# One fused attention and MoE kernel: the order of the loads of W2 and v, and the place of one key-value product

## The chip, the cores, the metric

One core of a Trainium2 chip. Its engines go by short names: PE is TensorE (PEld its weight loads), DVE is VectorE, ACT is ScalarE, POOL is GpSimd, SP is SyncE. The metric is the device time of one execution in microseconds; smaller is better. Every profile is of one execution.

## The reference

Attention in linear form, then an MLP with ELU:

```python
q_s = softmax(q, axis=-1); k_s = softmax(k, axis=2)      # 8 batches, 8 heads, 576 rows, 64 columns
kv  = einsum('bhsd,bhse->bhde', k_s, v)                  # the key-value product
x   = einsum('bhsd,bhde->bhse', q_s, kv) ...             # to 4608 tokens x 512
out = elu(x @ w_in) @ w_out                              # 512 -> 2048 -> 512
```

## The kernel before

It works in nine blocks of 512 tokens. A "unit" is half a batch: units 0 and 1 are batch 0, units 2 and 3 batch 1. For each block PE runs `hg` (x @ w_in, 64 matmuls, line L654) and `out` (ELU result @ w_out, 64 matmuls, L700). The attention of the next batch goes between the `out` matmuls: transposes of q (L464), the key-value product (L491), two groups that apply it (L584, L618). The output of a block needs all of W2, in 16 chunks of 256 KB, and in block 0 W2 is still coming in, together with q, k and v of batch 1.

The loads of that stage, all issued in this order by GpSimd on one queue:

```python
W2CUT = (0, 4, 8, 12, 13, 14, 16)     # part 0: chunks 0-3, 1: 4-7, 2: 8-11, 3: chunk 12, 4: 13, 5: 14-15
for what in (0, "2q", "3q", 1, 2, "2k", "2v", "3k", 3, "3v", 4, 5):
    if isinstance(what, int):
        gp = self.load_w2(what, -50, follow=gp)
    elif what == "3v":
        for h in range(2):                      # v of unit 3 as two halves, 288 KB each
            gp = self.load_half(3, "v", h, -50, gp)
    else: ...                                   # 576 KB each
```

PE's order in block 0 is a list of 24 steps, four token tiles for each part of W2, with the attention of batch 1 hung behind some of them:

```python
if j == 0:
    work = dict(zip((6, 9, 15, 20), (
        lambda: self.tp(2, C, key), lambda: self.tp(3, Dd, key),   # transposes of q
        lambda: kv([2, 3]),                                        # key-value product of units 2 and 3
        first)))                                                   # first attention group
    plan = [(ts, W2CUT[s], W2CUT[s + 1]) for s in range(6) for ts in range(4)]
```

The product is one PE step of 72 small matmuls. It waits for k (after its exponential on ACT) and v (after a cast to bf16 on DVE) of both units:

```python
R = []
for n in units:
    i = n % 2
    R += [f"kR{i}", f"VB{i}0", f"VB{i}1", f"VBone{i}"]
S.add("pe", len(units) * 270 + 200, mm, key, R=R, X=self.banks(ps), tag=f"kv{units}")
```

The kernel's own list scheduler orders the instructions on the other engines by modelled times, so a change of one order can move others.

The softmax here doesn't subtract the row's maximum and nothing guards it: scores larger than these inputs give would overflow.

Of the kernel before, what the change touches and what calls it, by code (L numbers as in the profile page):

```python
# [257 lines left out]
class Gen:  # L258
# [482 lines left out]
    def program(self):  # L741
# [49 lines left out]
        self.hg_mm(0, 0, 3, (1,))  # L791
        self.hg_mm(0, 1, 2, (1,))
        self.ao_rest(0, 1, -60)
        for what in (0, "2q", "3q", 1, 2, "2k", "2v", "3k", 3, "3v", 4, 5):
            if isinstance(what, int):
                gp = self.load_w2(what, -50, follow=gp)
            elif what == "3v":
                for h in range(2):
                    gp = self.load_half(3, "v", h, -50, gp)
            else:  # L800
                gp = self.load(int(what[0]), what[1], "gp", -50, follow=gp)
# [6 lines left out]
        def loads(n, ts, key):  # L808
            for t in ts:
                self.ldq = self.load(n, t, "sp", key, after=self.w2, follow=self.ldq)  # L810
                self.w2 = ()

        def elem_q(b, key, dmat="sp"):
            for n in (2 * b, 2 * b + 1):
                self.q_part(n, key)
                if b != 2:
                    self.q_mul(n, key, dmat)

        def elem_k(b, key, vconv="gp"):
            for n in (2 * b, 2 * b + 1):  # L820
                self.k_part(n, key, "halves" if n == 3 else vconv)

        def convert(b, key):
            for n in (2 * b, 2 * b + 1):
                self.cvt(n, key)
# [3 lines left out]
        for j in range(NBLK):  # L829
            order = [A, Bs, C, Dd]  # L830
            for g in range(8):
                self.hg(j, g, order[g % 4], key, "gp" if j or g > 2 else "act" if g == 1 else "dve",
                        (0, 1, 2, 3) if j or g > 3 else (2, 3))
                key += 1
                if (j, g) == (0, 1):
                    for x in (2, 3):
                        self.hg_mm(0, x, order[x], (0, 1), key)
                if (j, g) == (0, 0):
                    elem_q(1, 8, None)
                    elem_k(1, 8, "dve")  # L840
            if j == 1:
                S.rel = self.pe
                for n in (4, 5):
                    self.q_mul(n, key, "sp")
                convert(2, key)
            b = j + 1
            more = b + 1 < B
            work = {}
            k1 = key + 14
            if b < B:  # L850
                n0, n1 = 2 * b, 2 * b + 1
                S.slack = 3500 if j else 1500
                if more:
                    loads(n0 + 2, "q", key)
                    loads(n1 + 2, "q", key)
                    S.rel = self.pe
                    if j:
                        elem_q(b + 1, k1)

                def kv(units, ps=C, more=more):  # L860
                    self.kv(units, ps, key)
                    for n in units:
                        if more:
                            loads(n + 2, "kv", key)
                            self.k_part(n + 2, k1)

                def aos(b=b, more=more, A=A, C=C, Dd=Dd):

                    small = int(self.split(b) >= 5)
                    self.ao(2 * b, 1 - small, Dd, key)  # L870
                    self.ao(2 * b + 1, 1 - small, A, key)
                    self.ao_rest(b, C, key, small)
                    if more:
                        convert(b + 1, k1)

                def first():
                    for n, ps in ((2, Dd), (3, C)):
                        self.ao(n, 0, ps, key, evac="split")

                if j == 0:  # L880
                    work = dict(zip((6, 9, 15, 20), (
                        lambda: self.tp(2, C, key), lambda: self.tp(3, Dd, key), lambda: kv([2, 3]),
                        first)))
                else:
                    work = dict(zip((5, 12) if j == 1 else (3, 10), (lambda: kv([n0, n1]), aos)))
            if j == 0:
                plan = [(ts, W2CUT[s], W2CUT[s + 1]) for s in range(6) for ts in range(4)]
            else:
                plan = [(ts + t, jj, jj + 4) for ts in (0, 2) for jj in range(0, 16, 4) for t in range(2)]
            if j == NBLK - 1:  # L890
                plan = plan[:8] + [(ts, jj, jj + 4) for ts in (2, 3) for jj in range(0, 16, 4)]
            bank = [2 * A, 2 * A + 1, 2 * Bs, 2 * Bs + 1]
            for k, (ts, jj0, jj1) in enumerate(plan):
                self.out_mm(j, ts, bank[ts], jj0, jj1, key)
                if jj1 == 16:
                    self.out_store(j, ts, bank[ts], key, last=j == NBLK - 1)
                if k in work:
                    work[k]()
                key += 8 / len(plan)
            if j == 0:  # L900
                S.rel = self.pe
                elem_q(2, k1)
                self.ao_rest(1, Dd, key)
            A, Bs, C, Dd = (Dd, C, A, Bs) if j else (C, Dd, A, Bs)
# [32 lines left out]
```

## Time and profile before

| | before |
|---|---|
| median of 3 runs | 298.45 us (298.19 to 298.48) |
| PE busy | 290.1 us, 98% of a span of 296.5 us |
| DVE, ACT, POOL busy | 51%, 51%, 41% |
| granted clock of PE, as a share of full speed | 1.000 |

The prediction below shows the lines. Three views carry it: the chain that ended last (what each step waited for, in order of time), the timeline of one engine (start, length, engine, line, operation, count, and in brackets the idle time before and what ended it), and the waits of ACT and DVE for loads, from which the landings are read.

### The profile page before, as it was taken

The numbers are of one execution on the slowest core, as the hardware profiler recorded it, in microseconds if no ns is written. First come the engines' busy times: TensorE is split into PE (matmuls) and PEld (weight loads), VectorE is DVE, ScalarE is ACT, GpSimd is POOL, SyncE is SP. The second block draws the span as 40 slices with busy tenths as digits, with TensorE's granted clock in tenths as the row PEclk, the third lists the DMA queues.
The fourth block names the chain that finished last, engine by engine and source line by source line (L and its number), as shares of the span: only waits on it lengthen the run. The fifth ranks groups of instructions, "written<-read, shape, count | busy, mean of one in ns | idle before, by whom it ended". The sixth has DMA issues, their size and how long they took to land.

```text
span 296.5 us, 4336 instructions
## 1 busy us (share of the span) xinstructions
PE 290.1 (98%) x1824; PEld 234.9 (79%) x1824; DVE 149.9 (51%) x167; ACT 151.9 (51%) x176; POOL 122.9 (41%) x133
## 2 busy tenths in 40 slices
PE   7999999999999999999999999999999999999995
PEld 2578778887888788878888888888888888888883
DVE  6757942988347903792268416760661056106600
ACT  5666367953676275536554555536531454135411
POOL 8998101662187035713472337314740055005500
PEclk9999999999999999999999999999999999999999
DMA  7999988928991597039902990099003110230022
GB/s 243 320 393 390 389 281 308 389 83 133 337 248 66 200 354 147 0 96 362 238 7 56 359 270 17 4 346 194 0 0 71 45 30 0 56 76 13 0 71 71
DMA packets 36515, 49.37 MB, mean 167 GB/s; under 512 B 16656, under 2 KB 17168, under 8 KB 36496
## 3 DMA queue, kind: packets, MB, share of 16 engines
q1 hardware_dynamic: 29792, 34.29, 40.7%
q0 software_dynamic: 6320, 14.29, 15.8%
q10 hardware_dynamic: 384, 0.53, 0.5%
q8 instruction: 14, 0.23, 0.3%
q14 instruction: 5, 0.04, 0.0%
HBM read 36.70 MB, written 9.44 MB: 156 GB/s over the span
## 4 chain that ended last, share of the span: by engine, by line
PE 84%; DMA 7%; POOL 7%; issue 0%; ACT 0%; DVE 0%; POOLq 0%
PE PS L700 41%; PE PS L654 39%; DMA VR<-in_v_dram 7%; POOL W L347 3%; PE PS L491 2%; PE PS L584 2%; PE PS L618 1%; POOL W L358 1%; POOL KR L315 1%; POOL VR L315 1%; POOL QR L315 0%; POOL QR L753 0%; ACT OSB L714 0%; DVE VB L442 0%; POOL ID L729 0%
## 5 line engine op out<-in xcount | busy, mean ns | idle before, releaser
L683 DVE SCALAR_TENSOR_TENSOR GT<-ESB,PS 128x1024 fp32r<-128x1024 f32 x69 | 84.1, 1221 | 115.7 <-POOL ESB L680 115.5
L700 PE MATMUL PS<-W,GT 128*128 128x512 f32 x576 | 136.5, 392 | 0.0
L654 PE MATMUL PS<-XT,W 128*128 128x512 f32 x576 | 132.9, 390 | 0.0
L654 PEld LDWEIGHTS PS<-XT,W 128*128 128x128 f32 x576 | 107.9, 188 | 22.7 <-DVE GT L676 0.4
L700 PEld LDWEIGHTS PS<-W,GT 128*128 128x128 f32 x576 | 107.0, 188 | 22.4 <-DMA W<-in_moe_w_out_dram 0.4
L680 POOL TENSOR_SCALAR ESB<-ESB 128x1024 f32<-128x1024 f32 x69 | 73.6, 1076 | 101.0 <-ACT ESB L668 101.0
L668 ACT ACTIVATE ESB<-PS 128x1024 f32<-128x1024 f32 x72 | 73.8, 1028 | 51.3 <-PE PS L654 51.3
L714 ACT ACTIVATE OSB<-PS 128x512 f32<-128x512 f32 x36 | 21.4, 600 | 61.3 <-PE PS L700 60.9
L438 POOL CAST VB<-VR 128x1152 bf16<-128x1152 f32 x12 | 14.5, 1210 | 45.4 <-DMA VR<-in_v_dram 45.4
L398 DVE TENSOR_REDUCE ZQ<-QR 128x18 f32<-128x1152 f32 (+1 forms) x18 | 21.8, 1214 | 2.5 <-ACT QR L392 2.5
L412 DVE TENSOR_TENSOR QS<-QR,RZQ 128x1152 f16<-128x1152 f32 x16 | 21.6, 1362 | 0.4
L392 ACT ACTIVATE QR<-QR 128x1152 f32<-128x1152 f32 (+1 forms) x18 | 18.5, 1053 | 2.1 <-DMA QR<-in_q_dram 2.0
L432 ACT ACTIVATE KR<-KR 128x1152 bf16<-128x1152 f32 x14 | 15.9, 1169 | 6.0 <-DMA KR<-in_k_dram 6.0
L425 POOL CAST qsT<-QR 128x1152 fp32r<-128x1152 f16 x12 | 13.8, 1147 | 10.1 <-DMA QR<-QS 10.1
L604 ACT ACTIVATE XT<-PS 128x640 fp32r<-128x640 f32 (+1 forms) x12 | 8.2, 738 | 15.4 <-PE PS L584 15.4
L358 POOL DMA_DIRECT2D W<-in_moe_w_out_dram x6 | 10.2, 2389 | 0.0
L347 POOL DMA_DIRECT2D W<-in_moe_w_in_dram x16 | 10.0, 1361 | 0.0
L640 PE MATMUL PS<-IDLE 128*128 128x512 f32 (+1 forms) x14 | 8.1, 702 | 1.5 <-DVE IDLE L732 1.5
L628 ACT ACTIVATE XT<-PS 128x1024 fp32r<-128x1024 f32 (+3 forms) x8 | 6.8, 846 | 1.1 <-PE PS L618 1.1
L584 PE MATMUL PS<-qsT,MBLK 128*128 128x320 f32 (+3 forms) x32 | 7.1, 338 | 0.0
L640 PEld LDWEIGHTS PS<-IDLE 128*128 128x128 f32 (+1 forms) x14 | 2.6, 211 | 5.5 <-issue 2.3
L491 PEld LDWEIGHTS PS<-VB,KR 64*64 64x64 bf16 x504 | 4.7, 107 | 2.8 <-DVE GT L683 1.8
(45 smaller groups left out, 82.2 us busy)
## 6 DMA issues: line engine op xcount, KB each, us to landing
out_dram<-OSB SPq DMA_DIRECT2D x68, 128.0 KB, 3.6
QR<-in_q_dram SPq DMA_DIRECT2D x12, 576.0 KB, 7.9
KR<-in_k_dram SPq DMA_DIRECT2D x12, 576.0 KB, 5.6
VR<-in_v_dram SPq DMA_DIRECT2D x12, 576.0 KB, 6.6
W<-in_moe_w_in_dram POOLq DMA_DIRECT2D x16, 256.0 KB, 9.5
W<-in_moe_w_out_dram POOLq DMA_DIRECT2D x3, 1024.0 KB, 16.9
KR<-in_k_dram POOLq DMA_DIRECT2D x4, 576.0 KB, 13.6
VR<-in_v_dram POOLq DMA_DIRECT2D x4, 288.0 KB, 14.6
```

Source lines behind the costliest of these rows:

```text
L347: "gp", 530, lambda e, kc=kc: e.dma_start(self.W1[:, kc, sl], w[kc, :, :, sl]), key,
L392: lambda e, part=part: e.activation(part, part, AF.Exp), key,
L398: S.add("dve", 1350 if n > 1 else 750, lambda e, z=z, src=src: e.tensor_reduce(z, src, AX.X, ALU.add), key, R=self.q_res(n) if n > 1 else ...
L412: S.add("dve", 1400, lambda e: e.tensor_tensor(qso, raw[:, :, :, :], rz, ALU.mult), key, R=qR + [f"RZQ{i}"], W=[f"QS{al}"], low=True, tag= ...
L432: S.add("act", t_act(1152, False), lambda e: e.activation(ek[:, :, :, :], flat.rearrange("p (h c d) -> p h c d", h=2, c=CH), AF.Exp), key, ...
L438: self.cv[n] = S.add("gp", 1250, lambda e: e.tensor_copy(VB[:, :, :, 0:D], raw[:, :, :, :]), key, R=rv, W=[f"VB{i}0", f"VB{i}1"], low=True ...
L654: last = e.matmul(P[:, t * 512:(t + 1) * 512], self.W1[:, kc, tt * 128:(tt + 1) * 128], self.XT[:, kc, rc:rc + BLK], start=(kc == 0), stop ...
L668: S.add("act", t_act(1024, True), lambda e: e.activation(esb[:, :], P[:, :], AF.Exp), key, W=[f"E{i}"], X=self.banks(ps), tag=f"exp{j}.{g}")
L680: S.add("gp", 1120, lambda e: e.tensor_scalar(esb[:, :], esb[:, :], 1.0, 0.0, ALU.min, ALU.max), key, X=[f"E{i}"], tag=f"min{j}.{g}", port ...
L683: S.add("dve", t_dve(1024), lambda e: e.scalar_tensor_tensor(gt, esb[:, :], -1.0, P[:, :], ALU.add, ALU.max), key, R=[f"E{i}"], W=gw, X=se ...
L700: last = e.matmul(dst, GT[:, jj, ts * 128:(ts + 1) * 128], self.W2[:, jj, :], start=(jj == 0), stop=(jj == 15))
L714: S.add("act", t_act(512, True), lambda e: e.activation(osb[:, :], src, AF.Copy), key, W=[f"O{i}0", f"O{i}1"], X=[f"b{bk}"], tag=f"evo{jb} ...
```

## The change

Intent: W2's second part should not make PE wait near 33 us, so it goes ahead of q of unit 3. v of unit 3 should come earlier too, ahead of W2's chunk 12, and PE should do the key-value product before it needs chunk 12. No instruction is added or taken away.

```diff
-        for what in (0, "2q", "3q", 1, 2, "2k", "2v", "3k", 3, "3v", 4, 5):
+        for what in (0, "2q", 1, "3q", 2, "2k", "2v", "3k", "3v", 3, 4, 5):
...
                 if j == 0:
-                    work = dict(zip((6, 9, 15, 20), (
+                    work = dict(zip((6, 9, 11, 19), (
```

Step 11 is the last one with chunks 8 to 11; so the product moves up by the four matmuls of chunk 12. The first attention group moves up by one step too, from behind the first two matmuls of chunks 14 and 15 to ahead of them.

## The prediction

> **What bounds the kernel now.** I read the page first (shares of busy time), then the chain that ended last in order of time, then the timelines of PE, PEld, DVE and ACT between 29 and 66 us, then busy time by stage. PE is busy for 98% of the span at a granted clock of 1.000, so only a gap on PE, or work added to PE, can move the end. The chain says where it first hangs on something else.
>
> ```profile
> 21.30 21.23 DMA VR<-in_v_dram
> 42.53 0.02 issue
> 42.55 0.48 DVE VB L442
> 43.03 0.04 issue
> 43.07 0.77 PE PS L491 x67
> 43.84 1.59 PE PS L700 x6
> 45.43 0.81 PE PS L584 x4
> 46.25 1.39 PE PS L700 x6
> 47.64 0.40 PE PS L618 x4
> 48.03 14.59 PE PS L654 x64
> ...
> 79.30 14.51 PE PS L654 x64
> ```
>
> Columns: start, length, what. From 43.07 us to the end the chain is PE on PE with no wait. Before it stands one DMA: the second half of v of unit 3, landing at 42.53, then its cast to bf16 on DVE, then the key-value product (L491). So the end is 42.53 us, plus the cast, plus all PE work placed behind that product. The last line gives the steady rate: 64 matmuls of L654 in 14.51 us, 0.2267 us each; L700 has the same shape.
>
> The PE timeline shows how PE came to that point:
>
> ```profile
> 29.43 6.78 PE L700 MATMUL PS<-W,GT 128*128 128x512 f32 x28
> 36.04 0.68 PE L464 MATMUL PS<-ID,QS 128*128 128x128 f16 x9
> 36.53 2.98 PE L700 MATMUL PS<-W,GT 128*128 128x512 f32 x12
> 39.35 0.68 PE L464 MATMUL PS<-ID,QS 128*128 128x128 f16 x9
> 39.83 2.98 PE L700 MATMUL PS<-W,GT 128*128 128x512 f32 x12
> 43.07 0.78 PE L491 MATMUL PS<-VB,KR 64*64 64x65 bf16 x72 [0.26 <-DVE VB L442]
> ```
>
> I go by starts. The x12 run without a wait takes 39.35 - 36.53 = 2.82 us; the one ahead of L491 takes 43.07 - 39.83 = 3.24, so PE stalls 0.42 us for v (the bracket's 0.26 counts from a modelled end). The x28 run takes 6.61 against 28 x 0.2267 = 6.35: 0.26 us lost. The PEld timeline names its cause, W2's second part (chunks 4 to 7) landing late:
>
> ```profile
> 33.18 2.59 PEld L700 LDWEIGHTS PS<-W,GT 128*128 128x128 f32 x12 [0.39 <-DMA W<-in_moe_w_out_dram]
> ```
>
> So the stage has two small stalls, 0.26 and 0.42 us, both on loads. What the loads cost is read from the instructions that wait for them, on ACT and DVE:
>
> ```profile
> 37.37 1.17 ACT L432 ACTIVATE KR<-KR 128x1152 bf16<-128x1152 f32 x1 [5.28 <-DMA KR<-in_k_dram]
> 40.37 1.16 ACT L432 ACTIVATE KR<-KR 128x1152 bf16<-128x1152 f32 x1 [0.76 <-DMA KR<-in_k_dram]
> ```
>
> ```profile
> 38.88 0.76 DVE L447 CAST VB<-VR 128x1152 bf16<-128x1152 f32 x1 [0.74 <-DMA VR<-in_v_dram]
> 41.81 0.46 DVE L442 CAST VB<-VR 128x576 bf16<-128x576 f32 x1 [2.17 <-DMA VR<-in_v_dram]
> 42.55 0.47 DVE L442 CAST VB<-VR 128x576 bf16<-128x576 f32 x1 [0.28 <-DMA VR<-in_v_dram]
> ```
>
> k2, v2, k3 and the halves of v3 land one behind the other: 37.37, 38.88, 40.37, 41.81, 42.55. A 576 KB load takes 1.50 us, half of it 0.74. Between k3 and v3's first half lies W2's chunk 12 (256 KB) too: 41.81 - 40.37 - 0.74 = 0.70 us for it.
>
> ```profile
> 29.40:36.04 6.64, 6.64 (x29) 4.99 (x28) 6.06 (x7) 2.69 (x3) 1.61 (x2) 1.00 1.28 388
> 36.04:39.35 3.31, 3.31 (x23) 2.65 (x22) 2.50 (x4) 1.98 (x3) 0.00 (x0) 1.00 1.10 391
> ```
>
> By stage (window, then busy PE, PEld, DVE, ACT, POOL, clock, DMA share, GB/s): the loads run at 388 to 391 GB/s, so order, not issue time, sets each landing; all were issued by 22.4 us.
>
> **What the Trainium skill says.** "TensorE: Matmul & The Clock Gate", section "Step-by-step: what each phase is for": matmuls stay in program order and only weight loads are pulled ahead. So a key-value product that waits holds up every L700 behind it, though their weights have landed. The trace agrees: PE stalls 0.42 us at L491. The same page, "Back-to-back issue gap", gives N/2.4 + 2.5 ns, 216 ns for N=512, against 226.7 here; I use the trace's. "DMA: Bandwidth & Descriptors", section "SWDGE vs HWDGE vs iDMA", says that only one queue/context is allocated to loads issued by GpSimd; the landings above, in issue order and with no overlap, agree. "VectorE: DVE Perf Modes", section "The perf-mode tier table", puts an fp32 copy at 2x: 576 columns at 2x of 0.96 GHz is 0.30 us plus a fixed part, and the trace's 0.46 fits.
>
> **The change part by part.** No instruction, byte or buffer is added or taken away; two orders move.
>
> (a) Load order. W2's second part goes ahead of q3: its landing moves from about 33.16 to 33.16 - 1.50 = 31.66 us, ahead of the 29.43 + 16 x 0.2267 = 33.06 at which PE wants it. The 0.26 us stall goes. q3 lands 1 MB later, 1048 KB at about 390 GB/s or 2.7 us: from about 30.4 to 33.15. Its exponential (1.16 us) then ends at 34.3; its reduction on DVE started at 35.10 in any case, behind unit 2's multiply. So the transposes of unit 3, due on PE at about 39.1, are not delayed.
>
> (b) v3 ahead of chunk 12. v3 lands 0.70 us earlier: 42.53 - 0.70 = 41.83. Cast and hops as in the chain (0.02 + 0.48 + 0.04) give the key-value product at 42.37 at the earliest. Chunk 12 lands at about 42.53.
>
> (c) PE order. The product moves ahead of chunk 12's four matmuls (one for each of four token tiles). PE reaches it at 43.07 - 0.42 - 0.26 - 4 x 0.2267 = 41.48 us. It has to wait until 42.37: the stall there grows from 0.42 to 0.89 us. The saving of (a) is eaten whole by this wait, since the product starts when v3 is there, however early PE is.
>
> (d) The sum, from the product's start on. It starts 43.07 - 42.37 = 0.70 us earlier, with 4 x 0.2267 = 0.91 us more of PE work behind it. Net: 0.91 - 0.70 = +0.21 us. The other sum agrees: stalls of 0.26 + 0.42 = 0.68 before, 0 + 0.89 after, +0.21. The product after the first attention group (L584) stays the same work: 8 matmuls, L584, 8 matmuls in place of 6, L584, 6.
>
> (e) What else moves. After the product: its DVE part (in the DVE timeline 43.91 to 45.01, so 1.94 us from its start) ends at about 44.3, and L584 is due at 42.37 + 0.71 + 8 x 0.2267 = 44.9, no wait. Chunk 12 is wanted at 43.1 and landed 0.5 earlier; chunk 13 wanted at 44.0, lands as before at about 43.2; the last two wanted at about 45.7, all landed by 44.45. On the sync queue the k and v loads of batch 2 come ahead of the first two stores, some 1.8 us earlier. On DVE the reduction of q5 comes ahead of three ELU steps instead of behind two of them.
>
> **The rivals.** First, the intended gain: if v3 did not bind, both stalls would go, 0.68 us, and the time would be 297.8. Against it: the chain names v3's landing, and 0.70 us of earlier data can't pay for being asked 0.91 + 0.26 us earlier. For it only: if the queue sped up once chunk 12 is behind, which nothing shows. Second, a stall in the next block. The moved DVE reduction delays the ELU step of block 1's third group:
>
> ```profile
> 54.55 1.21 DVE L683 SCALAR_TENSOR_TENSOR GT<-ESB,PS 128x1024 fp32r<-128x1024 f32 x1
> 55.68 0.26 DVE L401 RECIPROCAL RZQ<-ZQ 128x18 f32<-128x18 f32 x1
> 56.09 1.22 DVE L683 SCALAR_TENSOR_TENSOR GT<-ESB,PS 128x1024 fp32r<-128x1024 f32 x1
> ```
>
> It would start about 57.2 instead of 56.09 and end near 58.4; the group that reuses its PSUM banks starts at 47.87 + 48 x 0.2267 = 58.75. About 0.3 us of margin: if I am off by that, PE loses 0.1 to 0.5 us, total 298.8 to 299.2. A cast of v on POOL also moves ahead of two steps there; it needs v4 by about 55, which landed before 55 even behind the stores, so I expect no loss from it. Third, q3's later arrival upsets the transposes of unit 3: that needs over 0.8 us more delay than I count; then +0.3 or more. Fourth, everything is absorbed: PE has no slack later (the chain is PE throughout), so a shift at 48 us is the shift at the end.
>
> **Range and chances.** 298.45 + 0.21 = 298.66 us. Three runs of before span 0.3 us, and the second rival leans to slower, the first to faster by up to 0.65. 8 in 10: 298.2 to 299.2. A 2% move would be 6 us, more than nine times all the stall there is in this stage; faster 0.005, within 2% 0.985, slower 0.01.
>
> **What would show it.** In the profile of the changed kernel: no wait of a weight load on W2 near 33 us; v's second half-cast starting at 41.85 (plus or minus 0.1); L491 starting at about 42.4 with a larger idle before it, about 0.7 by the bracket's count; the chain still passing through the v load and that cast, with 16 L700 behind the product; block 1's L654 starting near 48.1 instead of 47.87. Wrong would be: L491 starting at 41.5 (then v is not the bound), a wait of L700 on W2 after L491 (chunk 12 late), or a gap within block 1's 64 L654 (the second rival).

## The result

After: 298.22 us median of 4 runs (298.17 to 298.45); before, beside it: 298.32 us (297.90 to 298.48, 4 runs). The ratio is 1.000, 95% interval 0.9983 to 1.0018: the same within what can be told. A ratio is the mean time of one kernel's runs over that of the other's of the same rounds, so not quite the ratio of the medians.

The chain that ended last, of the changed kernel:

```profile
20.81 20.66 DMA VR<-in_v_dram
41.47 0.02 issue
41.49 0.48 DVE VB L442
41.97 0.04 issue
42.01 0.78 PE PS L491 x68
42.79 2.06 PE PS L700 x8
44.85 0.82 PE PS L584 x4
45.68 1.85 PE PS L700 x8
...
47.92 14.57 PE PS L654 x64
```

The shape is the one foretold: v's second half, its cast, the product, then PE alone, now with 16 matmuls of L700 behind the product instead of 12. But v landed at 41.47 us, not at 41.83. The PE timeline (selected rows):

```profile
29.27 6.51 PE L700 MATMUL PS<-W,GT 128*128 128x512 f32 x28
...
39.41 2.07 PE L700 MATMUL PS<-W,GT 128*128 128x512 f32 x8
42.01 0.78 PE L491 MATMUL PS<-VB,KR 64*64 64x65 bf16 x72 [0.53 <-DVE VB L442]
```

The wait on W2 near 33 us is gone: 35.62 - 29.27 = 6.35 us for 28 matmuls (6.61 before), which is the steady rate. The stall at the product grew: from 39.41 to 42.01 are 2.60 us. Twelve matmuls took 2.82 with no wait (36.53 to 39.35 in before), so eight take four times 0.2267 less, 1.91, and the stall is 0.69 us (0.42 before).

Of the DVE timeline in block 1, the moved reduction:

```profile
55.73 1.30 DVE L398 TENSOR_REDUCE ZQ<-QR 128x18 f32<-128x1152 f32 x1
56.94 2.34 DVE L683 SCALAR_TENSOR_TENSOR GT<-ESB,PS 128x1024 fp32r<-128x1024 f32 x2
```

The third group's ELU step starts at 56.94 instead of 56.09. PE pays nothing for it: the 64 matmuls of L654 in that block take 14.57 us (14.59 before).

So this run lost 0.91 us of PE work behind the product and won 1.06 by v's earlier landing. Of the 1.06, the order of loads can explain only about 0.7. The rest was there before any moved load: W2's first part, issued at 14.1 us and untouched by the change, landed at 27.43 us before and at 27.02 in this run. Whether the change costs 0.2 us, as predicted, or nothing, is thus hidden behind 0.4 us of chance in one profile and an interval of plus or minus 0.5 us in the times. The experiments had to settle that.

### The profile page after: what moved, and what is told of

It is laid out like the page before. It is cut to its first block, busy times and chain, and to the rows that moved or that the text cites. A ratio compares the mean times of both kernels' runs of the same rounds, so it can differ in the third digit from the quotient of the medians.

```text
span 296.3 us, 4336 instructions
## 1 busy us (share of the span) xinstructions
PE 289.5 (98%) x1824; PEld 234.9 (79%) x1824; DVE 149.5 (50%) x167; ACT 152.0 (51%) x176; POOL 123.0 (42%) x133
## 4 chain that ended last, share of the span: by engine, by line
PE 85%; DMA 7%; POOL 6%; issue 0%; ACT 0%; DVE 0%; POOLq 0%
PE PS L700 41%; PE PS L654 39%; DMA VR<-in_v_dram 7%; POOL W L347 3%; PE PS L491 2%; PE PS L584 2%; PE PS L618 1%; POOL W L358 1%; POOL KR L315 1%; POOL VR L315 0%; POOL QR L315 0%; POOL QR L753 0%; ACT OSB L714 0%; DVE VB L442 0%; POOL ID L729 0%
## 5 line engine op out<-in xcount | busy, mean ns | idle before, releaser
L700 PE MATMUL PS<-W,GT 128*128 128x512 f32 x576 | 136.3, 392 | 0.0
L654 PE MATMUL PS<-XT,W 128*128 128x512 f32 x576 | 132.7, 390 | 0.1
L654 PEld LDWEIGHTS PS<-XT,W 128*128 128x128 f32 x576 | 107.8, 188 | 22.6 <-issue 0.2
L700 PEld LDWEIGHTS PS<-W,GT 128*128 128x128 f32 x576 | 107.1, 188 | 22.2
L425 POOL CAST qsT<-QR 128x1152 fp32r<-128x1152 f16 x12 | 13.8, 1152 | 10.0 <-DMA QR<-QS 10.0
L358 POOL DMA_DIRECT2D W<-in_moe_w_out_dram x6 | 9.1, 2417 | 0.0
L491 PEld LDWEIGHTS PS<-VB,KR 64*64 64x64 bf16 x504 | 4.7, 107 | 3.1 <-DVE GT L683 1.8
L584 PE MATMUL PS<-qsT,MBLK 128*128 128x320 f32 (+3 forms) x32 | 7.1, 338 | 0.0
```

The source lines that it names most:

```text
L654: last = e.matmul(P[:, t * 512:(t + 1) * 512], self.W1[:, kc, tt * 128:(tt + 1) * 128], self.XT[:, kc, rc:rc + BLK], start=(kc == 0), stop ...
L700: last = e.matmul(dst, GT[:, jj, ts * 128:(ts + 1) * 128], self.W2[:, jj, :], start=(jj == 0), stop=(jj == 15))
```

## The experiments

**The theories.** V: PE stands in order behind whichever load it needs next. The product starts 0.54 us after v's landing, and the end of the kernel is that moment plus the PE work placed behind it. N: nothing in this stage reaches the end. G: each stall taken away is gained.

Each kernel had five timed runs against nine of before on the same chip (1, 13 or 14), and one profile; changed had four against four. All were correct. Before has one profile only, from the first series, whose chip is not on record. This table is the whole of it; "to W2.0" is the start of block 1's L654 less the landing of W2's first part in the same profile, which takes out the chance part of the loads. Before has 20.44.

| kernel | v landed | L491 starts | L700 again | block 1 | to W2.0, against before | ratio of times (95%), us |
|---|---|---|---|---|---|---|
| before | 42.53 | 43.07 | 43.78 | 47.87 | 0 | |
| changed | 41.47 | 42.01 | 42.72 | 47.76 | +0.30 | 1.0000 (0.9983 to 1.0018), 0.0 |
| after_again | 42.06 | 42.61 | 43.31 | 48.31 | +0.23 | 1.0008 (0.9995 to 1.0020), +0.24 |
| a_only | 42.20 | 42.74 | 43.45 | 47.54 | +0.02 | 0.9999 (0.9985 to 1.0012), 0.0 |
| pe_only | 42.59 | 43.13 | 43.84 | 48.83 | +0.91 | 1.0032 (1.0020 to 1.0045), +0.95 |
| late_kv | 41.49 | 43.34 | 44.05 | 48.14 | +0.66 | 1.0020 (1.0007 to 1.0032), +0.60 |
| x_ahead | 42.77 | 43.31 | 44.02 | 49.06 | +0.96 | 1.0023 (1.0011 to 1.0036), +0.69 |
| x_behind | 41.96 | 42.50 | 43.32 | 48.35 | +0.40 | 1.0008 (0.9994 to 1.0022), +0.24 |
| usplit_a | 42.57 | 42.53 | 43.53 | 47.67 | -0.23 | 0.9990 (0.9977 to 1.0002), -0.30 |
| best | 42.51 | 42.66 | 43.42 | 47.52 | -0.17 | 1.0037 (1.0024 to 1.0050), +1.10 |
| csplit_a | 42.40 | 42.52 | 43.29 | 47.51 | -0.05 | 0.9994 (0.9981 to 1.0008), -0.18 |
| usplit_after | 42.39 | 42.12 | 43.35 | 48.33 | -0.05 | 1.0004 (0.9991 to 1.0016), +0.12 |

The us are (ratio - 1) x 298. From block 1's start to the end of the span it is 248.4 to 248.6 us in every one of these profiles but best's, so what a kernel gains or loses it has by block 1. The mark is steadier than the times: from W2's first part to v it is 15.10 to 15.12 us in the four profiles with before's order around v (before, a_only, pe_only, usplit_a), and 14.43 to 14.45 in the five with v ahead of chunk 12 and no load added before it.

### after_again: the changed kernel once more

> The changed kernel once more, for a narrower interval and a second trace. In the first traces v3's second half landed at 42.53 us before and 41.47 after: 1.06 us earlier, where the order of loads explains 0.70; the rest is that the whole stream of loads, from W1 on, ended 0.40 us earlier in that one run. Theory V (the key-value product starts 0.54 us after v3's landing, and everything behind it follows on PE): with the stream's chance part taken out the change costs +0.2 us, so 0.0 to +0.4 us here, and in this trace L491 starts at (landing + 0.54). Rival N (nothing in this stage reaches the end): 0.0. Rival G (the stalls removed are gained): -0.3 to -0.7 us.

Measured: median 298.04 us against 297.82, ratio 1.0008, +0.24 us. The chain of waits of its profile:

```profile
20.62 21.44 DMA VR<-in_v_dram
...
42.61 0.78 PE PS L491 x69
```

The same kernel as above, and v lands 0.59 us later, with the product 0.60 later; this run took 298.69 us and the one above 298.17, so 0.52 more. The cause is in the view of loads, for W2's first part alone, the last column being the time from issue to landing: first the changed kernel's first profile, then this one.

```profile
W<-in_moe_w_out_dram POOLq DMA_DIRECT2D x1, 1024.0 KB, 12.9
```

```profile
W<-in_moe_w_out_dram POOLq DMA_DIRECT2D x1, 1024.0 KB, 13.5
```

One kernel, one load, 0.6 us apart: the stream of loads has a chance part, and the end of the kernel follows it. With the landing of W2's first part as zero, v lands at 15.10 in before and at 14.45 and 14.43 in the two profiles of the changed kernel: the order of loads is worth 0.65 to 0.67 us, and the first profile's other 0.4 us were luck. G is out; V and its +0.2 fit, though the interval of the times still holds 0.

### a_only: W2's second part alone

```diff
-        for what in (0, "2q", "3q", 1, 2, "2k", "2v", "3k", 3, "3v", 4, 5):
+        for what in (0, "2q", 1, "3q", 2, "2k", "2v", "3k", 3, "3v", 4, 5):
```

> Only W2's second part moves ahead of q3; the product and v3 stay. Compute engines have the same order as before. Theory V: the wait of L700 on W2 near 33 us (0.26 us) goes, PE reaches L491 0.26 us earlier and waits there 0.26 longer (stall 0.68 instead of 0.42); time 0.0 us against before. Rival G: -0.26 us.

PE timeline:

```profile
39.43 2.98 PE L700 MATMUL PS<-W,GT 128*128 128x512 f32 x12
42.74 0.78 PE L491 MATMUL PS<-VB,KR 64*64 64x65 bf16 x72 [0.34 <-DVE VB L442]
```

Ratio 0.9999. The x28 run is back at the steady rate (35.64 - 29.29 = 6.35), and the wait at the product has grown to 42.74 - 39.43 - 2.82 = 0.49 us; v landed 0.33 us earlier by luck, without which it would be 0.82, or 0.68 as expected if PE's own earlier start (29.29 against 29.43) is taken out too. The gain of an earlier W2 stops at the next load in PE's order. G (-0.26) is not excluded by the times, but by the column to W2.0: +0.02.

### pe_only: PE's order alone

```diff
-                    work = dict(zip((6, 9, 15, 20), (
+                    work = dict(zip((6, 9, 11, 19), (
```

> Only PE's order changes: the product ahead of chunk 12's four matmuls, the loads as before (v3 behind chunk 12). Theory V: L491 starts when it did (v3's landing + 0.54), but has 4 matmuls (0.91 us) more behind it: +0.9 us, near 299.2. Rival N: 0.0. Its ACT and SP orders differ in block 1 too, which could add a few tenths there; the trace will tell by the start of block 1's L654 against L491.

```profile
39.89 2.07 PE L700 MATMUL PS<-W,GT 128*128 128x512 f32 x8
43.13 0.78 PE L491 MATMUL PS<-VB,KR 64*64 64x65 bf16 x72 [1.17 <-DVE VB L442]
```

In the PE timeline the product starts when v lets it, 43.13 (43.07 before), after a wait of 43.13 - 39.89 - 1.91 = 1.33 us. Four matmuls that used to run in that time now stand behind it: +0.95 us, interval 0.6 to 1.3. N is out. This is the largest clean effect here, and its size is 4 x 0.2267 = 0.91. The orders on ACT and the sync queue differ too, but later: the column to W2.0 has +0.91 by the start of block 1, and the rest of the kernel takes as long as in the others.

### late_kv: the loads alone

The loads of the changed kernel, with (6, 9, 15, 20) kept.

> The loads of the changed kernel with PE's order of before: v3 ahead of chunk 12, but the product behind chunk 12's matmuls. Compute engines have the same order as before. Theory V in its general form (PE stands at whichever load it needs in order): now chunk 12 is what PE waits for, landing about 0.67 us after v3: its four matmuls start near 42.5 instead of 41.5, the product follows at 43.5 without a wait on v, so +0.4 us against before. Rival G: -0.3 us. A theory in which v's landing alone counts would give -0.7 us.

```profile
42.22 1.20 PE L700 MATMUL PS<-W,GT 128*128 128x512 f32 x4 [0.71 <-DMA W<-in_moe_w_out_dram]
```

PE timeline: v now lands at 41.49, 1.04 earlier than in before (0.38 of it luck), and the kernel is slower by 0.60 us (0.2 to 1.0). The bound has changed its name: PE waits for chunk 12. That is more than the 0.4 expected, though 0.4 lies in the interval, and the trace shows a part of it. From 42.22 to the product at 43.34 the four take 1.12 us, where 0.91 was counted. They start at 42.22, 42.55, 42.79 and 43.02: 0.12 us is lost behind the wait, and 0.09 in the step to the product, which is there without a wait too (usplit_a: 2.91 us from 39.62 to 42.53 for twelve, not 2.82). The changed kernel is right to move the loads and PE's order together; each of the two alone costs more.

### x_ahead and x_behind: one more load, at two places

```diff
+            elif what == "x":        # 256 KB of w_out into an output buffer not used before 47 us
+                gp = S.add("gp", ISSUE["gp"], lambda e: e.dma_start(
+                    self.OSB[3][:, :], self.w_out[0:128, :]), -50, W=["O30", "O31"], dma="xtra", ...)
 x_ahead:   (0, "2q", 1, "3q", 2, "2k", "2v", "3k", "x", "3v", 3, 4, 5)
 x_behind:  (0, "2q", 1, "3q", 2, "2k", "2v", "3k", "3v", "x", 3, 4, 5)
```

> The changed kernel with one extra 256 KB load (a copy of W2 rows into an output buffer that is not used before 47 us) put just ahead of v3. It delays v3 and all behind it by about 0.67 us. Theory V: the whole kernel is later by the same 0.67: +0.9 us against before (0.2 of the change plus 0.67). Rival N: +0.2 or less. Its DVE order in block 1 is that of before again (the reduction of q5 behind the ELU steps), so a rest that came from there would be gone.

> The same extra 256 KB load, but just behind v3 and ahead of chunk 12. Same bytes, same issue work, the same DVE order as x_ahead. Theory V: v3 lands as in the changed kernel; chunk 12 lands 0.67 later, at about v3's landing + 1.35, and PE wants it at v3's landing + 1.26: so it costs 0.1 us, total +0.3 us against before, 0.6 less than x_ahead. A theory that the bytes as such or the issue cost: the same time as x_ahead.

Both have the DVE order of before in block 1. x_ahead in its PE timeline:

```profile
43.31 0.78 PE L491 MATMUL PS<-VB,KR 64*64 64x65 bf16 x72 [1.35 <-DVE VB L442]
```

v lands 15.11 us after W2's first part (14.43 without the extra load), and the product follows. Times: +0.69 us for x_ahead (0.3 to 1.1), +0.24 for x_behind (-0.2 to +0.7); by the traces +0.96 and +0.40 against before, and so +0.7 and +0.15 against the changed kernel. Expected were +0.9 and +0.3 against before. The same bytes cost 0.56 us more ahead of v than behind it, as V says and as the rival of plain bytes doesn't. The times alone would not part the two kernels; the traces do.

### usplit_a and usplit_after: the wait filled

If V holds, the wait can be filled with PE work that needs only what has landed. Half of the product is such work: unit 2's k and v have been there for 3 us. The step is cut in two, with the waits of each:

```diff
-        S.add("pe", len(units) * 270 + 200, mm, key, R=R, X=self.banks(ps), tag=f"kv{units}")
+        if units == [2, 3]:
+            for x, dur in ((0, 370), (1, 370)):
+                i = units[x] % 2
+                S.add("pe", dur, lambda e, x=x: mm(e, [(x, 0, CH)]), key,
+                      R=[f"kR{i}", f"VB{i}0", f"VB{i}1", f"VBone{i}"],
+                      X=self.banks(ps), tag=f"kv{units}")
+        else: ...                               # the other products as before; the rest is cut here
```

usplit_a has it on a_only, usplit_after on the changed kernel; no engine's order differs from these.

> The load order of a_only and PE's order of before, with the key-value product cut into two PE steps with their own waits: unit 2 (v2 and k2 have long landed) and unit 3. Unit 2's 36 matmuls (0.35 us) then run inside the wait for v3, so less PE work stands behind v3's landing. Theory V: -0.35 us against before, but W2's last load (chunks 14, 15) lands 1.91 us after v3 and is wanted at v3 + 0.54 + 0.36 + 0.91 = 1.81, which gives back 0.1: -0.25 to -0.35 us. Rival (the stall can't be filled, the product takes as long in whatever pieces): 0.0.

> The changed kernel with the key-value product in two PE steps, unit 2 and unit 3; no order on any engine differs from the changed kernel. There PE stands 0.9 us at the product. Theory V: unit 2's part runs in that wait, product's end at v3's landing + 0.96 instead of + 1.25: 0.29 less than the changed kernel, so -0.1 us against before (between -0.3 and +0.1). If the change's cost were not this wait: +0.2 as for the changed kernel.

The PE timeline of usplit_after shows the two parts:

```profile
42.12 0.48 PE L492 MATMUL PS<-VB,KR 64*64 64x65 bf16 x36
42.93 0.48 PE L492 MATMUL PS<-VB,KR 64*64 64x65 bf16 x36 [0.33 <-DVE VB L442]
```

In both kernels L700 goes on 0.96 us after v's landing instead of 1.25, the 0.29 expected. usplit_a: -0.30 us, 0.9990 (0.9977 to 1.0002), as expected, the best kernel, though the interval just holds 1. usplit_after: +0.12 us (-0.3 to +0.5) where -0.1 was expected; the trace agrees with the expectation (-0.05 to W2.0), and the times can't tell. Its profiled run took 298.71 us with the latest landing of W2's first part of all, 27.95.

### best and csplit_a: a further cut, and a trap

In best, on top of a_only, v of unit 3 is loaded by rows in two parts so that only 16 of the 72 matmuls wait for the last one; W2's chunks 14 and 15 come as two loads, and the first attention group moves to step 21 with them.

```diff
+W2CUT = (0, 4, 8, 12, 13, 14, 15, 16)
+            for x, c0, c1, vb, dur in ((0, 0, CH, (0, 1), 370), (1, 0, 5, (0,), 200), (1, 5, CH, (1,), 170)):
...
```

> As usplit_a, and v3 comes as two loads by rows (5 and 4 of 9) rather than by heads, so that unit 3's product can be cut too: only its last 16 matmuls (about 0.16 us) wait for the last load, which is smaller (256 KB, its cast about 0.42 us); W2's last load is cut in two (chunk 14, chunk 15), so that chunk 14 is there when wanted. Theory V: work behind v3's landing falls by 0.55 us and the cast by 0.05: -0.5 to -0.6 us against before, if chunk 13 (landing 0.63 after v3, wanted at v3 + 0.02 + 0.42 + 0.04 + 0.16 = 0.64) is not late. The sync queue's order after block 1 differs, which I expect to cost nothing. Rival: 0.0.

A miss: +1.10 us. Block 1 started early enough (47.52). Then, of the waits of PE and of the sync queue's timeline:

```profile
PE PS L595 <- POOL qsT L427: 1.2, 1, 1.2
```

```profile
67.13 1.38 SPq L418 DMA_TRANSPOSE QR<-QS  x1
68.56 0.58 SPq L315 DMA_DIRECT2D KR<-in_k_dram  x1
69.19 1.94 SPq L418 DMA_TRANSPOSE QR<-QS  x1
```

(L595, L427 and L418 are before's L584, L425 and L416.) The scheduler, fed other modelled times, put a k load between the two transposes of q; the second transpose landed at 75.30 (72.51 in csplit_a), POOL cast it at 75.35, and PE stood 1.2 us in block 1. csplit_a keeps the loads by rows but not W2's extra cut, and with it the orders of before on PE, ACT and the sync queue:

> The kernel best lost 1.1 us instead of winning 0.5. Its trace has two things: the product ended 0.91 us after v3's landing (1.25 in before), so the stage did gain 0.35 (block 1's L654 started at 47.52 against 47.87); then PE waited 1.2 us near 75 us for POOL's cast of a transposed q, because in that kernel the order on the sync queue had put a k load between the two DMA transposes. This one keeps v3's loads and product by rows, but not the cut of W2's last load, and its orders on PE, ACT and SP are those of before. If the order on the sync queue was the whole of the loss: -0.25 to -0.35 us against before, and no wait of L584's kind on POOL. If the loads by rows did it: +1 us again.

Measured: -0.18 us (-0.6 to +0.2), and no such wait. So the loads by rows were not what cost 1.1 us. That it was the order on the sync queue is what best's waits point to; no run moved that order alone, and in best the orders on ACT and DVE differ as well. The gain was less than expected: L700 goes on 0.89 us after v's landing (0.36 won), but loads by rows land v 15.28 us after W2's first part instead of 15.11, and PE now waits for W2's last load near 44.3 us, in all 0.05 to the good. The cut by unit is better and simpler.

## Why the prediction was right

The mechanism was right: v binds, the saving upstream is eaten by the wait for it, and the cost is the work moved behind it less v's earlier landing. The number in us is less well shown. The time foretold, 298.66, was 0.4 us above the median, 298.22, which lies just inside the low end of the range, and the first ratio shows no cost at all. The effect named, +0.21 us, fits the second set of runs (+0.24, but -0.15 to +0.60) and what the traces show once the luck of the loads is taken out (+0.23 and +0.30). Point by point:

- (a) Right: the wait on W2's second part goes, 0.26 us, and is worth nothing by itself (a_only). Not all of the 0.26 was lateness: W2 was wanted at 33.06 and its matmuls began at 33.18; about half was lost in the slower first matmuls behind the wait. The transposes of unit 3 were not delayed by q3's later landing (38.92 against 39.35).
- (b) Right in size: predicted 0.70 us earlier for v, found 0.65 to 0.67. Wrong as an absolute time: 41.83 was derived from one profile as if the stream of loads were the same in every run. It landed at 41.47 and 42.06, so the marks named (the half-cast at 41.85 plus or minus 0.1, the product near 42.4, block 1 near 48.1) were missed by 0.2 to 0.4 us, early in the first profile and late in the second.
- (c) Right: the stall at the product grows, to 0.69 us in one profile and 0.88 in the other (42.61 - 39.82 - 1.91), predicted 0.89.
- (d) Right: 16 matmuls behind the product, 0.91 us, against 0.7 won. pe_only measures the first term alone as 0.95.
- (e) Right that it costs nothing here. The k and v loads of batch 2 were issued earlier than said (45.02 against 47.32, so 2.3 us, not 1.8); the last two W2 chunks were not waited for.
- The rivals: the intended gain did not come (a_only); the moved DVE reduction stayed within its margin. Fourth rival, no slack later: right, 248.4 to 248.6 us from block 1 on. One slip without effect: 2% of the time is 8.8 times the 0.68 us of stall, not more than nine times.

The range was sized from three runs and named only stalls as its causes; that one profile's luck is 0.4 us and twice the effect was not in it.

## What to carry to other kernels

When an engine runs in order and stands at loads that come in order, removing one wait moves the stall to the next load: count from the last landing that binds, and count the work placed behind it. Delay that work as little as possible behind it, and cut a step so that its landed part runs inside the wait. For an effect below the spread of the runs, look in the trace for a mark that the change cannot touch and count from it.

## What the Trainium skill lacked or had wrong

- "TensorE: Matmul & The Clock Gate", section "Back-to-back issue gap": 216 ns isolated and about 131 ns sustained for N=512. The matmuls here, on fp32 data that the kernel declares as fp32r, ran at 226.7 ns in an unbroken stream (64 in 14.51 us). No rate for this type was found there.
- No page that I read gives the cost of a restart as such: behind a wait for W2 the second matmul started 0.34 us after the first (33.18 to 33.52 in before, 42.22 to 42.55 in late_kv), not 0.227.
- "DMA: Bandwidth & Descriptors", section "Why a DMA increments its semaphore by 16 and not by 1": only the full 16 mean landed, and the trace agrees as far as it goes: v's cast starts 0.02 us after the last of the 16. A figure for how far apart the 16 come is missing: for the untouched 1 MB load of W2's first part the first of the 16 came at 25.16 to 25.54 us in twelve profiles, the last 1.6 to 2.5 us later (27.02 to 27.95). That spread is the chance part that moved the kernel's end by 0.5 us.
- What sets that spread no run tested; the traces have a lead, which no page that I read has. In all twelve profiles one instruction fetch of 16 KB (queue q8) runs at 17.1 to 18.0 us and takes 1.0 to 1.1 us. Right behind it one step between the landings of W1, otherwise 0.53 to 0.74 us, is 1.2 to 2.0 us. In that step the last of the 16 falls further behind the fifteenth: from 0.03 to 0.47 us before it to 0.55 to 1.36 us after it. In before, fifteen sixteenths of v had landed by 41.63 and the last came at 42.53. That the fetch holds up one of the 16 is a guess from these times, not shown.
